# A decode layer on one core: the identity of the fold matmuls loaded once for eight, and w_down in blocks of 88, 96 and 128 partitions

## The chip, the core and the metric

The kernel runs on one core of a Trainium2 chip. The core has a matrix engine (TensorE, PE; its weight loads are shown on a row of their own, PEld), a vector engine (DVE), a scalar engine (ACT), GpSimd (POOL) and SyncE (SP), which here only issues DMAs. Sixteen DMA engines move data from the chip's memory (HBM) into the on-chip memory of 128 partitions. The engines run side by side and wait for each other by semaphores. The metric is the device time of one execution in microseconds (us), taken as the median of several runs.

## What is computed

One decode step (one token, width 640) of an attention block with cached keys and values, and a gated MLP behind it. Cut to what matters:

```python
def _A_ref(x, k_cache, v_cache, wq, wo):           # 32 heads of 128, 4096 cached positions
    q = (x @ wq).reshape(B, Sq, Hq, Dh).transpose(0, 2, 1, 3)
    scores = jnp.einsum("bhqd,bhkd->bhqk", q, k) * (Dh ** -0.5)
    p = _softmax(scores, axis=-1)
    o = jnp.einsum("bhqk,bhkd->bhqd", p, v)
    return o.transpose(0, 2, 1, 3).reshape(B, Sq, Hq * Dh) @ wo

def _B_ref(x, w_gate, w_up, w_down):               # 640 -> 1728 -> 640
    g = jnp.einsum("bsd,df->bsf", x, w_gate)
    u = jnp.einsum("bsd,df->bsf", x, w_up)
    h = _gelu(g) * u
    return jnp.einsum("bsf,fd->bsd", h, w_down)

h = x + _A_ref(_layernorm(x), A_k_cache, A_v_cache, A_wq, A_wo)
h2 = h + _B_ref(_layernorm(h), B_w_gate, B_w_up, B_w_down)
```

All inputs are bf16. Keys and values are 33.6 MB each, wq and wo 5.2 MB each, w_gate, w_up and w_down 2.2 MB each: 84.2 MB, each byte used once.

## The kernel before

The program is written out instruction by instruction: a small class (`Sched`) collects the operations of each engine in the order in which they are to run, with the semaphore values that each waits for, and emits them at the end. Nothing reorders them afterwards.

**Loads.** All large loads are issued from SP, in one order: wq; K of groups 0 and 1; V of group 0; then V and K of the further groups in turn; wo in two parts with the last V between them; w_gate, w_up; w_down; at the end the result. The 32 heads are worked in eight groups of four. A group's K (4 MB, two buffers `kbuf`) has 128 partitions, 32 for each head, with 128 positions in each; V likewise (`vbuf`). A load waits for its buffer: K's for the last product of the group two before, V's for the last value matmul of the group two before. The MLP's weights lie in the buffers that the caches leave: w_gate and w_up in `kbuf`, w_down (`wd_sb`) in `vbuf`.

**Scores.** For each group there are four pieces of 32 positions. `mult` (L339) multiplies K by the query on DVE, 128 x 4096 elements into `prod` (three buffers). `fold` (L348) sums over the head's 128 elements, 16 at a time: eight matmuls with the identity `Ibf` as the stationary operand add eight slices of `prod` into one PSUM bank `pf`. Each of the eight is a weight load of the same identity and a matmul. `red` (L355) sums the remaining 16 on DVE. `top`, `turn`, `head` and `soft` make the softmax's maximum and the exponentials (ACT, L384). `values` (L395) multiplies by V, `extract` (L410, L413) and `column` (L418) bring the result into columns, `project` (L601) multiplies by wo. The last group takes its values in `values_last` (L403).

**MLP.** `up` (L648) makes one column of 128 hidden units per matmul group: for each of the five slices of the input (`NC_D`) and each of the `NF` = 14 columns one matmul with 128 x 128 weights, first for w_gate (`pg`), then for w_up (`pu`). The columns follow the layout of w_down: `WD_PARTS` = (5, 4, 3, 1) are blocks of 128 partitions in which each partition holds 5, 4, 3 or 1 consecutive rows of w_down, 13 columns (`NFT`) in all, 1664 rows. The 14th column is the last 128 hidden units, of which 64 (`FREM`) are not in the others. Their 64 rows of w_down come in eight small loads (L581), each of four partitions with two rows (`NRR`) of 640 elements, to partitions of `wd_sb` that POOL has set to zero (L577). Since these rows lie otherwise than the column of hidden units, the column is brought to their places by L666 on DVE, a small matmul L670 (`rest`) and a copy L672, with the help of `hsum`, `hrow` and `hcol`, made in the prologue (L225 to L232).

The hidden units go through the GELU on DVE and ACT (L655 to L664) into `hm`. `down` (L686) then multiplies: for each of 15 columns of `wd_sb` four matmuls of 160 output elements each, into four partition quarters of `pd`, in the order: blocks of 5 and 4, the two of the small loads, blocks of 3 and 1. The small matmul L670 comes after the first five columns. L690 copies the result, L692 stores it.

Of the kernel before, what the change touches and what calls it, by code (L numbers as in the profile page):

```python
# [5 lines left out]
FP32 = mybir.dt.float32  # L6
BF16 = mybir.dt.bfloat16
ALU = mybir.AluOpType
ACTF = mybir.ActivationFunctionType
AX = mybir.AxisListType  # L10

D = 640
H = 32
DH = 128
SK = 4096
DF = 1728
# [7 lines left out]
NG = H // HG  # L24
# [6 lines left out]
NW = 4  # L31
HW = H // NW
DJ = 128 // HW
NFT = 13
NF = NFT + 1
WD_PARTS = (5, 4, 3, 1)

WD_COLS = []
for _n in WD_PARTS:
    _b = 128 * len(WD_COLS)  # L40
    WD_COLS += [(_b, _n, _i) for _i in range(_n)]
FREM = DF - NFT * 128
NRR = 2
NRP = FREM // NRR // 2
NRK = 32 + NRP
WIDE = 32


# [65 lines left out]
def bass_sequential_preLN__gqa_block_cached__glu_gated_geglu__decode_kernel(  # L114
# [12 lines left out]
    S = Sched(nc)  # L127

    def sb(name, shape, dt):
        return nc.alloc_sbuf_tensor(name, shape, dt)  # L130
# [5 lines left out]
    vbuf = [sb("vbuf%d" % i, [128, R, DH], BF16) for i in range(2)]  # L136

    def over(name, base, shape):
        return nc.alloc_sbuf_tensor_at(name, shape, BF16, offset=nc.lookup_mloc(base).addr)
# [2 lines left out]
    wo_sb = over("wo_sb", arena, [128, NW, HW, D])  # L142
    wg_sb = over("wg_sb", kbuf[NG % 2], [128, NC_D, DF])
    wu_sb = over("wu_sb", kbuf[(NG + 1) % 2], [128, NC_D, DF])
    wd_sb = over("wd_sb", vbuf[NG % 2], [128, NFT + NRR, D])

    NPR = 3
    prod = [sb("prod%d" % i, [128, RP, DH], BF16) for i in range(NPR)]
# [33 lines left out]
    r_t = sb("r_t", [128, NF], FP32)  # L182
    gu = sb("gu", [128, NF], FP32)
    hm = sb("hm", [128, NF], BF16)
    hq = sb("hq", [128, NRR], BF16)
    hr = sb("hr", [128, NRR], BF16)
    hcol = sb("hcol", [128, NRR], FP32)
    hrow = sb("hrow", [128, 128], BF16)
    o_sb = sb("o_sb", [128, D // 4], BF16)
    hx = sb("hx", [128, 32, NC_D], FP32)  # L190
    m32 = sb("m32", [128, 32], FP32)
# [2 lines left out]
    part = sb("part", [128, 128], FP32)  # L194
    eps = sb("eps", [128, 1], FP32)
    ones_bf = sb("ones_bf", [128, 128], BF16)
    I32 = sb("I32", [128, 128], FP32)
    Ibf = sb("Ibf", [128, 128], BF16)
    pf = [nc.alloc_psum_tensor("pf%d" % i, [128, 512], FP32) for i in range(2)]
# [3 lines left out]
    pz = nc.alloc_psum_tensor("pz", [128, 512], FP32)  # L203
# [17 lines left out]

    t_e4 = S.op("vector", lambda v: v.reduce_sum(
        e4[:, :], I32[:, :].rearrange("p (j i) -> p j i", j=4), axis=AX.X), [t_i32])
    hsum = hx[:, :, :].rearrange("p a b -> p (a b)")[:, 0:2 * NRP]
    t_hsum = S.op("vector", lambda v: v.reduce_sum(  # L225
        hsum, I32[:, 128 - FREM:128].rearrange("p (r i) -> p r i", i=NRR), axis=AX.X))
    t_hrow = S.op("vector", lambda v: v.memset(hrow[:, :], 0.0))
    t_hrow = S.op("vector", lambda v: v.tensor_copy(
        hrow[:, 0:64].rearrange("p (b r) -> p b r", b=2)[:, :, 0:NRP],
        hsum.rearrange("p (b r) -> p b r", b=2)), [t_hsum, t_hrow])  # L230
    t_hcol = S.op("vector", lambda v: v.reduce_sum(
        hcol[:, :], I32[:, 128 - FREM:128].rearrange("p (r i) -> p i r", i=NRR), axis=AX.X))  # L232
    t_m32 = S.op("vector", lambda v: v.reduce_sum(
        m32[:, :], I32[:, :].rearrange("p (j i) -> p i j", j=4), axis=AX.X))
    S.op("vector", lambda v: v.reduce_sum(
# [3 lines left out]
    a = S.op("vector", lambda v: v.reduce_sum(  # L239
        jred[:, :], I32[:, :].rearrange("p (j c) -> p j c", c=HW), axis=AX.X))  # L240
    b = S.op("vector", lambda v: v.reduce_sum(
        cred[:, :], I32[:, :].rearrange("p (j c) -> p c j", c=HW), axis=AX.X))
# [11 lines left out]
    kfree, vfree = [None] * NG, [None] * NG  # L254
# [45 lines left out]
    a = None  # L300
    for c in range(NC_D):
        a = S.op("tensor", lambda t, c=c: t.matmul(
            pm[:, c:c + 1], x_sb[0:1, c::NC_D], ones_bf[0:1, 0:1],
            start=(c == 0), stop=(c == NC_D - 1), skip_group_check=True),
            [d_x, t_onebf], token=(c == NC_D - 1))
# [23 lines left out]
    fold_done, red_done = {}, {}  # L329
# [7 lines left out]
    def mult(g, s):  # L337
# [3 lines left out]
            in1=qb[:, g, :].unsqueeze(1).to_broadcast([128, RP, DH]), op=ALU.mult),  # L341
            [d_k[g], t_qb[g], fold_done.get(n - NPR)])

    def fold(g, s, t_mult):
        n = g * NP + s
        W = 512 // RP
        for j in range(DH // W):
            fold_done[n] = S.op("tensor", lambda t, j=j: t.matmul(  # L348
                pf[n % 2][:, :], Ibf[:, :], prod[n % NPR][:, :, j * W:(j + 1) * W],
                start=(j == 0), stop=(j == DH // W - 1)),  # L350
                [t_mult, t_ibf, red_done.get(n - 2)], token=(j == DH // W - 1))

    def red(g, s):
# [99 lines left out]
    for n in range(NG - 1):  # L453
        w = (n - 3) // 2 if n >= 3 and n % 2 else None
        p, o = n - 1, n - 2
# [60 lines left out]
    g = NG - 1  # L516
    w = NW - 1
    p, o = g - 1, g - 2
# [45 lines left out]
    def load_wo(lo, hi):  # L564
# [9 lines left out]
                  [0, 5], [kfree[NG - 2]])  # L574
    d_wu = pieces("wu", wu_sb, B_w_up[:, :].rearrange("(p c) n -> p c n", c=NC_D),
                  [0, 5], [kfree[NG - 1]])
    t_zr = S.op("gpsimd", lambda g: g.memset(wd_sb[0:64, NFT:NFT + NRR, :], 0.0), [vfree[NG - 2]])  # L577
    rows = B_w_down[NFT * 128:DF, :].rearrange("(b e j i) n -> b j e i n", b=2, j=4, i=NRR)
    for h in range(2):
        for j in range(4):  # L580
            d_wdr = S.dma("sync", "wdr", lambda s, h=h, j=j: s.dma_start(  # L581
                wd_sb[32 * h + j:32 * h + NRP:4, NFT:NFT + NRR, :], rows[h, j]), [t_zr])
    d_wd = []
    for i, n in enumerate(WD_PARTS):
        s0 = len(d_wd)
        tok = S.dma("sync", "wd%d" % i, lambda s, s0=s0, n=n: s.dma_start(
            wd_sb[:, s0:s0 + n, :],
            B_w_down[128 * s0:128 * (s0 + n), :].rearrange("(p i) n -> p i n", i=n)), [vfree[NG - 2]])
        d_wd += [tok] * n
    d_wd += [d_wdr] * NRR  # L590


    pp = pf[0]
# [14 lines left out]
    for i in range(w - 1):  # L608
# [8 lines left out]
    b = project(w)  # L617
    t_h = S.op("vector", lambda v: v.scalar_tensor_tensor(
        out=h32[:, :], in0=x32[:, :], scalar=1.0, in1=pp[:, 0:NC_D * WIDE:WIDE], op0=ALU.mult, op1=ALU.add,
# [3 lines left out]
    pd = pf[1]  # L623
    NQ = D // 4
# [13 lines left out]
    def up(ps, w, d_w):  # L638
        b = None
        for c in range(NC_D):  # L640
            for s in range(NF):
                first = c == 0 and s == 0
                last = c == NC_D - 1 and s == NF - 1
                part = w[:, c, DF - 128:DF]
                if s < NFT:
                    b0, n, k = WD_COLS[s]
                    part = w[:, c, b0 + k:b0 + 128 * n:n]
                b = S.op("tensor", lambda t, s=s, c=c, part=part, first=first, last=last: t.matmul(  # L648
                    ps[:, s * WIDE:(s + 1) * WIDE], part, hln[:, c:c + 1].to_broadcast([128, WIDE]),
                    start=first, stop=last, skip_group_check=True), [t_hln, d_w[c]], token=last)  # L650
        return b
# [3 lines left out]
    a = S.op("vector", lambda v: v.tensor_copy(g_t[:, :], pg[:, 0:NF * WIDE:WIDE]), [t_g])  # L655
    a = S.op("vector", lambda v: v.tensor_mul(t1[:, :], g_t[:, :], g_t[:, :]), [a])
    a = S.op("vector", lambda v: v.tensor_mul(t2[:, :], t1[:, :], g_t[:, :]), [a])
    a = S.op("vector", lambda v: v.scalar_tensor_tensor(
        out=t3[:, :], in0=t2[:, :], scalar=GELU_C1, in1=g_t[:, :], op0=ALU.mult, op1=ALU.add), [a])
    a = S.op("scalar", lambda a: a.activation(e_t[:, :], t3[:, :], ACTF.Exp, scale=-2.0 * GELU_C0), [a])  # L660
    a = S.op("vector", lambda v: v.tensor_scalar(d_t[:, :], e_t[:, :], 1.0, 0.0, ALU.add, ALU.add), [a])
    a = S.op("vector", lambda v: v.reciprocal(r_t[:, :], d_t[:, :]), [a])
    a = S.op("vector", lambda v: v.tensor_mul(gu[:, :], g_t[:, :], r_t[:, :]), [a])
    t_hm = S.op("vector", lambda v: v.tensor_mul(hm[:, :], gu[:, :], pu[:, 0:NF * WIDE:WIDE]), [a, t_u])  # L664

    a = S.op("vector", lambda v: v.tensor_tensor(  # L666
        out=hq[:, :], in0=hcol[:, :], in1=hm[:, NFT:NF].to_broadcast([128, NRR]), op=ALU.mult), [t_hm, t_hcol])

    def rest():
        b = S.op("tensor", lambda t: t.matmul(  # L670
            pz[:, 32:32 + NRR], hrow[:, :], hq[:, :], start=True, stop=True), [a, t_hrow])
        return S.op("vector", lambda v: v.tensor_copy(hr[:, :], pz[:, 32:32 + NRR]), [b])  # L672

    def down(s, j):
        if s >= NFT:
            return hr[0:NRK, s - NFT:s - NFT + 1], wd_sb[0:NRK, s, j * NQ:(j + 1) * NQ]
        return hm[:, s:s + 1], wd_sb[:, s, j * NQ:(j + 1) * NQ]

    n = sum(WD_PARTS[0:2])
    order = list(range(n)) + list(range(NFT, NFT + NRR)) + list(range(n, NFT))  # L680
    for i, s in enumerate(order):
        if s == WD_PARTS[0]:
            t_hr = rest()
        for j in range(4):
            last = i == len(order) - 1
            b = S.op("tensor", lambda t, s=s, j=j, last=last: t.matmul(  # L686
                pd[32 * j:32 * j + 1, 0:NQ], *down(s, j),
                start=False, stop=last, skip_group_check=True),
                [t_hr if s >= NFT else t_hm, d_wd[s]], token=(last and j == 3))
    t_o = S.op("vector", lambda v: v.tensor_copy(o_sb[:, :], pd[:, 0:NQ]), [b])  # L690
    d_o = S.dma("sync", "out", lambda s: s.dma_start(
        out[0, 0, :].rearrange("(j i) -> j i", j=4), o_sb[0:128:32, :]), [t_o])  # L692
# [32 lines left out]
```

## Time and profile before

| what | value |
|---|---|
| median of 3 runs | 203.9 us (203.71 to 204.09) |
| span of the profiled execution | 202.3 us |
| TensorE busy | 155.4 us (77%), weight loads 71.0 us (35%) |
| DVE busy | 116.4 us (58%) |
| ACT, POOL busy | 30.7 us, 2.4 us |
| read from HBM | 84.23 MB, 416 GB/s over the span |
| mean granted TensorE clock | 0.930 |
| eight fold matmuls (L348) at the full clock | 1.85 us |
| issue of the eight small loads on SP | 5.10 us, from 175.80 |
| issue of the four large w_down loads | 1.86 us, from 180.94 |

The span runs from the first to the last instruction of one profiled execution; the runs' time has some 1.6 us more around it. Busy shares are means over very different stages: up to some 167 us the groups of K and V pass through, then wo and the MLP's weights come in while TensorE works in short stretches with waits between. The granted clock is 1.00 for most of the first part and 0.50 from 181 us to the end.

### The profile page before, as it was taken

The page shows a single profiled execution, that of the slowest core. Times are in us where ns is not written, and L with a number is a line of the kernel's source. Part 1 is how long each engine was busy: PE and PEld are TensorE (multiplying, and loading weights), DVE is VectorE, ACT ScalarE, POOL GpSimd, SP SyncE. Part 2 cuts the span into 40 slices and gives each one's busy share as a digit, 9 for nine tenths or more (in the row PEclk, how much of TensorE's full clock was granted, in tenths as well). Part 3 has the DMA queues.
Part 4 walks back from the last instruction along what each step waited for, and adds up shares of the span by engine and source line. Part 5 has one row for each costly group of instructions (what it writes and reads, how often), then busy time and mean ns, then how long its engine had stood idle before and what let it go on. Part 6 is the DMA issues. An engine that isn't in the chain of part 4 may idle for free.

```text
span 202.3 us, 2515 instructions
## 1 busy us (share of the span) xinstructions
PE 155.4 (77%) x1084; PEld 71.0 (35%) x1084; DVE 116.4 (58%) x153; ACT 30.7 (15%) x110; POOL 2.4 (1%) x8
## 2 busy tenths in 40 slices
PE   1005349689959997996899499979777999978675
PEld 1001013233323432432343134324323344667562
DVE  6200087998097919953993488569999513301121
ACT  2002200007000600420060004200604004000000
POOL 1000000000000000000000000000000000200000
PEclk9999999999979999999999979999999999985555
DMA  7999999999999999999999999999999899999993
GB/s 259 437 437 415 421 441 473 428 415 415 418 453 460 421 416 415 424 449 447 428 428 415 424 447 447 421 434 415 428 444 441 380 429 461 441 383 437 434 388 117
DMA packets 3940, 84.38 MB, mean 417 GB/s; under 512 B 441, under 2 KB 570, under 8 KB 986
## 3 DMA queue, kind: packets, MB, share of 16 engines
q1 hardware_dynamic: 3928, 84.23, 97.4%
q8 instruction: 8, 0.13, 0.3%
q14 instruction: 2, 0.02, 0.0%
q10 hardware_dynamic: 2, 0.00, 0.0%
HBM read 84.23 MB, written 0.00 MB: 416 GB/s over the span
## 4 chain that ended last, share of the span: by engine, by line
DMA 59%; DVE 24%; PE 15%; issue 1%; SPq 0%; DVEq 0%
DMA kbuf<-in_A_k_cache_dram 46%; DVE prod L339 16%; DMA wu_sb<-in_B_w_up_dram 13%; PE pf L348 8%; PE pu L395 4%; DVE sc L355 3%; DVE xz L413 2%; PE pu L648 1%; DVE xm L410 1%; PE pf L686 1%; PE pg L395 1%; DVE mx L363 0%; DVE mrow L372 0%; PE pm L367 0%; SPq L247 0%
## 5 line engine op out<-in xcount | busy, mean ns | idle before, releaser
L339 DVE TENSOR_TENSOR prod<-kbuf,qb 128x4096 bf16<-128x4096 bf16 x32 | 72.8, 2278 | 45.0 <-DMA kbuf<-in_A_k_cache_dram 45.0
L348 PE MATMUL pf<-prod,Ibf 128*128 128x512 bf16 x256 | 66.5, 408 | 23.0 <-DVE prod L339 22.9
L348 PEld LDWEIGHTS pf<-prod,Ibf 128*128 128x128 bf16 x256 | 24.4, 103 | 62.3 <-DVE prod L339 29.5
L395 PE MATMUL pg<-vbuf,P 128*16 128x512 bf16 x128 | 29.9, 379 | 0.0
L355 DVE TENSOR_REDUCE sc<-pf 128x32 f32<-128x512 f32 x32 | 21.6, 676 | 4.8 <-PE pf L348 4.7
L395 PE MATMUL pu<-vbuf,P 128*16 128x512 bf16 x96 | 22.2, 379 | 0.0
L318 PE MATMUL pq<-wq_sb,xb 128*128 128x512 bf16 x40 | 12.1, 441 | 12.3 <-DMA wq_sb<-in_A_wq_dram 11.1
L380 ACT ACTIVATE nb<-pm 128x4 f32<-128x4 f32 x8 | 1.4, 175 | 118.5 <-PE pm L377 118.5
L384 ACT ACTIVATE P<-sc,nb 32x128 bf16<-32x128 f32 x32 | 18.6, 580 | 0.9
L395 PEld LDWEIGHTS pg<-vbuf,P 128*16 128x16 bf16 x128 | 10.6, 89 | 14.5 <-issue 1.3
L395 PEld LDWEIGHTS pu<-vbuf,P 128*16 128x16 bf16 x96 | 8.1, 90 | 11.7 <-issue 1.7
L324 ACT CAST qb<-pq 32x128 bf16<-32x128 f32 x32 | 8.2, 258 | 15.8 <-PE pq L318 15.0
L318 PEld LDWEIGHTS pq<-wq_sb,xb 128*128 128x128 bf16 x40 | 3.8, 110 | 17.1 <-issue 12.8
L384 ACT ACTIVATION_READ_ACCUMULATOR P<-sc,nb 32x1 f32 x32 | 8.0, 251 | 0.0
L601 PE MATMUL pf<-aP,wo_sb 128*128 128x32 bf16 x160 | 7.1, 194 | 0.8 <-issue 0.6
L413 DVE TENSOR_REDUCE xz<-xm 16x128 f32<-16x512 f32 x7 | 7.3, 1044 | 0.2
L601 PEld LDWEIGHTS pf<-aP,wo_sb 128*128 128x128 bf16 x160 | 6.8, 131 | 1.5 <-issue 1.1
L403 PE MATMUL pq<-P,vbuf 128*128 128x32 bf16 x128 | 3.6, 188 | 1.4 <-DMA vbuf<-in_A_v_cache_dram 1.4
L410 DVE TENSOR_TENSOR xm<-pg,rmask 16x512 f32<-16x512 f32 x4 | 2.7, 670 | 3.4 <-PE pg L395 3.4
L293 ACT ACTIVATE ln<-pz,ln 128x1 f32<-128x1 f32 x2 | 0.5, 263 | 23.9 <-DVE ln L290 23.9
L403 PEld LDWEIGHTS pq<-P,vbuf 128*128 128x128 bf16 x128 | 3.5, 104 | 1.5 <-DMA vbuf<-in_A_v_cache_dram 1.5
L410 DVE TENSOR_TENSOR xm<-pu,rmask 16x512 f32<-16x512 f32 x3 | 1.9, 643 | 3.2 <-PE pu L395 3.2
(84 smaller groups left out, 56.4 us busy)
## 6 DMA issues: line engine op xcount, KB each, us to landing
kbuf<-in_A_k_cache_dram SPq DMA_DIRECT2D x8, 4096.0 KB, 25.2
vbuf<-in_A_v_cache_dram SPq DMA_DIRECT2D x8, 4096.0 KB, 22.8
wq_sb<-in_A_wq_dram SPq DMA_DIRECT2D x1, 5120.0 KB, 15.1
wo_sb<-in_A_wo_dram SPq DMA_DIRECT2D x1, 3840.0 KB, 28.7
wg_sb<-in_B_w_gate_dram SPq DMA_DIRECT2D x1, 2160.0 KB, 22.5
wu_sb<-in_B_w_up_dram SPq DMA_DIRECT2D x1, 2160.0 KB, 27.1
wo_sb<-in_A_wo_dram SPq DMA_DIRECT2D x1, 1280.0 KB, 17.8
wd_sb<-in_B_w_down_dram SPq DMA_DIRECT2D x1, 800.0 KB, 15.8
```

Source lines behind the costliest of these rows:

```text
L318: tok = S.op("tensor", lambda t, c=c, n0=n0: t.matmul(pq[:, :], xb[:, c, :], wq_sb[:, c, n0:n0 + HG * DH], start=(c == 0), stop=(c == NC_D ...
L324: t_qb[g] = S.op("scalar", lambda a, lo=lo, hi=hi, hh=hh: a.copy(qb[lo:hi, g, :], pq[lo:hi, hh * DH:(hh + 1) * DH]), [tok])
L339: return S.op("vector", lambda v: v.tensor_tensor(out=prod[n % NPR][:, :, :], in0=kbuf[g % 2][:, s * RP:(s + 1) * RP, :], in1=qb[:, g, :]. ...
L348: fold_done[n] = S.op("tensor", lambda t, j=j: t.matmul(pf[n % 2][:, :], Ibf[:, :], prod[n % NPR][:, :, j * W:(j + 1) * W], start=(j == 0) ...
L355: red_done[n] = S.op("vector", lambda v: v.reduce_sum(sc[g % 2][:, s * RP:(s + 1) * RP], pf[n % 2][:, :].rearrange("p (r w) -> p r w", r=R ...
L384: t_exp[g] = S.op("scalar", lambda a, lo=lo, hi=hi, h=h, hh=hh: a.activation(P4[g % 2][lo:hi, :, hh], sc[g % 2][lo:hi, :], ACTF.Exp, bias= ...
L395: t_pv[g] = S.op("tensor", lambda t, i=i, r=r, last=last: t.matmul(pv[g % 2][0:VM, :], P4[g % 2][:, r:r + VR, :], vbuf[g % 2][:, r:r + VR, :],
L403: t_pv[g] = S.op("tensor", lambda t, r=r: t.matmul(pq[:, 0:WIDE], vbuf[g % 2][:, r, :], P4[g % 2][:, r, :].unsqueeze(1).to_broadcast([128, ...
L410: a = S.op("vector", lambda v: v.tensor_tensor(out=xm[:, :, :], in0=pv[g % 2][0:VM, :].rearrange("p (r d) -> p r d", r=VR), in1=rmask[:, : ...
L413: t_ext[g] = S.op("vector", lambda v: v.reduce_sum(xz[g % 2][:, :], xm[:, :, :].rearrange("p r d -> p d r"), axis=AX.X), [a, t_acc[g - 2] ...
L601: tok = S.op("tensor", lambda t, c=c, cc=cc, first=first, last=last: t.matmul(pp[:, cc * WIDE:(cc + 1) * WIDE], wo_sb[:, w, c, cc::NC_D], ...
L648: b = S.op("tensor", lambda t, s=s, c=c, part=part, first=first, last=last: t.matmul(ps[:, s * WIDE:(s + 1) * WIDE], part, hln[:, c:c + 1] ...
```

## The change

Two things are changed.

In `fold` only the first of the eight matmuls brings its weights. The seven others are made as instructions by hand, with the flag that no weights are loaded, and use those that are there.

w_down is cut otherwise: a block of 88 partitions with four consecutive rows in each, one of 96 with one row, and blocks of 128 with 4, 3, 2 and 1 rows: 15 columns, 1728 rows. The 64 rows in eight small loads, POOL's memset, the rearranging of their hidden units (L666, L670, L672) and what the prologue prepares for it are gone. `up` works 15 columns with 128 weights each as before; of a column with 88 or 96 rows the rest of the result isn't read. `down` takes the columns in the order in which they are loaded, with 88, 96 or 128 partitions.

```diff
-NFT = 13
-NF = NFT + 1
-WD_PARTS = (5, 4, 3, 1)
+WD_PARTS = ((88, 4), (96, 1), (128, 4), (128, 3), (128, 2), (128, 1))
 
 WD_COLS = []
-for _n in WD_PARTS:
-    _b = 128 * len(WD_COLS)
-    WD_COLS += [(_b, _n, _i) for _i in range(_n)]
-FREM = DF - NFT * 128
-NRR = 2
-NRP = FREM // NRR // 2
-NRK = 32 + NRP
+_b = 0
+for _p, _n in WD_PARTS:
+    WD_COLS += [(_b, _n, _i, _p) for _i in range(_n)]
+    _b += _p * _n
+assert _b == DF
+NF = len(WD_COLS)
...
+    def again(t, out, lhsT, rhs, stop):
+        m = mybir.InstMatmult(
+            name=nc.get_next_instruction_name(), engine=mybir.EngineType.PE,
+            ins=[t.lower_ap(rhs), t.lower_ap(lhsT, for_matmul_weights=True)], outs=[t.lower_ap(out)],
+            start_tensor_calc=False, stop_tensor_calc=stop,
+            tile_size=(128, 128), tile_position=(0, 0), ldweights=False)
+        return t.add_instruction(m)
+
     def fold(g, s, t_mult):
...
-            fold_done[n] = S.op("tensor", lambda t, j=j: t.matmul(
-                pf[n % 2][:, :], Ibf[:, :], prod[n % NPR][:, :, j * W:(j + 1) * W],
-                start=(j == 0), stop=(j == DH // W - 1)),
+            def mm(t, j=j):
+                dst, src = pf[n % 2][:, :], prod[n % NPR][:, :, j * W:(j + 1) * W]
+                if j == 0:
+                    return t.matmul(dst, Ibf[:, :], src, start=True, stop=False)
+                return again(t, dst, Ibf[:, :], src, j == DH // W - 1)
+            fold_done[n] = S.op("tensor", mm,
                 [t_mult, t_ibf, red_done.get(n - 2)], token=(j == DH // W - 1))
...
-    t_zr = S.op("gpsimd", lambda g: g.memset(wd_sb[0:64, NFT:NFT + NRR, :], 0.0), [vfree[NG - 2]])
-    rows = B_w_down[NFT * 128:DF, :].rearrange("(b e j i) n -> b j e i n", b=2, j=4, i=NRR)
-    for h in range(2):
-        for j in range(4):
-            d_wdr = S.dma("sync", "wdr", lambda s, h=h, j=j: s.dma_start(
-                wd_sb[32 * h + j:32 * h + NRP:4, NFT:NFT + NRR, :], rows[h, j]), [t_zr])
     d_wd = []
-    for i, n in enumerate(WD_PARTS):
+    for i, (p, n) in enumerate(WD_PARTS):
         s0 = len(d_wd)
-        tok = S.dma("sync", "wd%d" % i, lambda s, s0=s0, n=n: s.dma_start(
-            wd_sb[:, s0:s0 + n, :],
-            B_w_down[128 * s0:128 * (s0 + n), :].rearrange("(p i) n -> p i n", i=n)), [vfree[NG - 2]])
+        b0 = WD_COLS[s0][0]
+        tok = S.dma("sync", "wd%d" % i, lambda s, s0=s0, b0=b0, p=p, n=n: s.dma_start(
+            wd_sb[0:p, s0:s0 + n, :],
+            B_w_down[b0:b0 + p * n, :].rearrange("(p i) n -> p i n", i=n)), [vfree[NG - 2]])
         d_wd += [tok] * n
-    d_wd += [d_wdr] * NRR
...
-                part = w[:, c, DF - 128:DF]
-                if s < NFT:
-                    b0, n, k = WD_COLS[s]
-                    part = w[:, c, b0 + k:b0 + 128 * n:n]
+                b0, n, k, _ = WD_COLS[s]
+                part = w[:, c, b0 + k:b0 + 128 * n:n]
...
-    n = sum(WD_PARTS[0:2])
-    order = list(range(n)) + list(range(NFT, NFT + NRR)) + list(range(n, NFT))
-    for i, s in enumerate(order):
-        if s == WD_PARTS[0]:
-            t_hr = rest()
+    for s, (_, _, _, p) in enumerate(WD_COLS):
         for j in range(4):
-            last = i == len(order) - 1
-            b = S.op("tensor", lambda t, s=s, j=j, last=last: t.matmul(
-                pd[32 * j:32 * j + 1, 0:NQ], *down(s, j),
+            last = s == NF - 1
+            b = S.op("tensor", lambda t, s=s, j=j, p=p, last=last: t.matmul(
+                pd[32 * j:32 * j + 1, 0:NQ], hm[0:p, s:s + 1], wd_sb[0:p, s, j * NQ:(j + 1) * NQ],
                 start=False, stop=last, skip_group_check=True),
-                [t_hr if s >= NFT else t_hm, d_wd[s]], token=(last and j == 3))
+                [t_hm, d_wd[s]], token=(last and j == 3))
```

More of the change, by code (lines that the diff above doesn't have):

```diff
@@ L144, in bass_sequential_preLN__gqa_block_cached__glu_gated_geglu__decode_kernel @@
     wu_sb = over("wu_sb", kbuf[(NG + 1) % 2], [128, NC_D, DF])
-    wd_sb = over("wd_sb", vbuf[NG % 2], [128, NFT + NRR, D])
+    wd_sb = over("wd_sb", vbuf[NG % 2], [128, NF, D])
     NPR = 3
@@ L184, in bass_sequential_preLN__gqa_block_cached__glu_gated_geglu__decode_kernel @@
     hm = sb("hm", [128, NF], BF16)
[L185 to L188, printed above, removed]
     o_sb = sb("o_sb", [128, D // 4], BF16)
@@ L223, in bass_sequential_preLN__gqa_block_cached__glu_gated_geglu__decode_kernel @@
         e4[:, :], I32[:, :].rearrange("p (j i) -> p j i", j=4), axis=AX.X), [t_i32])
[L224 to L232, printed above, removed]
     t_m32 = S.op("vector", lambda v: v.reduce_sum(
@@ L664, in bass_sequential_preLN__gqa_block_cached__glu_gated_geglu__decode_kernel @@
     t_hm = S.op("vector", lambda v: v.tensor_mul(hm[:, :], gu[:, :], pu[:, 0:NF * WIDE:WIDE]), [a, t_u])
[L666 to L677, printed above, removed]
-    n = sum(WD_PARTS[0:2])
-    order = list(range(n)) + list(range(NFT, NFT + NRR)) + list(range(n, NFT))
-    for i, s in enumerate(order):
-        if s == WD_PARTS[0]:
-            t_hr = rest()
+    for s, (_, _, _, p) in enumerate(WD_COLS):
         for j in range(4):
-            last = i == len(order) - 1
-            b = S.op("tensor", lambda t, s=s, j=j, last=last: t.matmul(
-                pd[32 * j:32 * j + 1, 0:NQ], *down(s, j),
+            last = s == NF - 1
+            b = S.op("tensor", lambda t, s=s, j=j, p=p, last=last: t.matmul(
+                pd[32 * j:32 * j + 1, 0:NQ], hm[0:p, s:s + 1], wd_sb[0:p, s, j * NQ:(j + 1) * NQ],
                 start=False, stop=last, skip_group_check=True),
-                [t_hr if s >= NFT else t_hm, d_wd[s]], token=(last and j == 3))
+                [t_hm, d_wd[s]], token=(last and j == 3))
     t_o = S.op("vector", lambda v: v.tensor_copy(o_sb[:, :], pd[:, 0:NQ]), [b])
```

## The prediction

> **What bounds the kernel now.** I read the page first: share of span, DMA row, queues.
>
> ```profile
> span 202.3 us, 2515 instructions
> ...
> DMA  7999999999999999999999999999999899999993
> ...
> DMA packets 3940, 84.38 MB, mean 417 GB/s; under 512 B 441, under 2 KB 570, under 8 KB 986
> ...
> q1 hardware_dynamic: 3928, 84.23, 97.4%
> q8 instruction: 8, 0.13, 0.3%
> ```
>
> SP's queue keeps the sixteen DMA engines busy 97.4% of the span, and no slice between the first and the last is below 8 tenths. The weights and caches come in one queue, in order: what lands last is set by the bytes of the slowest engine, not by when a load is issued. The DMA issues show the same: w_down's loads land 15.8 to 17.6 us after issue, because they stand behind w_up.
>
> Next the timeline of the end, weight loads of TensorE (start, us, what, in brackets the idle time before and its releaser):
>
> ```profile
> 194.84 2.42 PEld L648 LDWEIGHTS pu<-hln,wu_sb 128*128 128x128 bf16 x70 [1.52 <-DMA wu_sb<-in_B_w_up_dram]
> 197.69 0.49 PEld L686 LDWEIGHTS pf<-wd_sb,hm 128*1 128x1 bf16 x20 [0.44 <-DVE hm L664]
> 198.46 0.10 PEld L670 LDWEIGHTS pz<-hq,hrow 128*128 128x128 bf16 x1 [0.27 <-issue]
> 198.57 0.36 PEld L686 LDWEIGHTS pf<-wd_sb,hm 128*1 128x1 bf16 x16
> 199.20 0.10 PEld L686 LDWEIGHTS pf<-wd_sb,hr 48*1 48x1 bf16 x8 [0.27 <-issue]
> 199.57 0.23 PEld L686 LDWEIGHTS pf<-wd_sb,hm 128*1 128x1 bf16 x12 [0.26 <-DMA wd_sb<-in_B_w_down_dram]
> 199.94 0.09 PEld L686 LDWEIGHTS pf<-wd_sb,hm 128*1 128x1 bf16 x4 [0.15 <-DMA wd_sb<-in_B_w_down_dram]
> ```
>
> w_up's landing at 194.84 starts `pu`, and the last four matmuls of the down product wait for the last block of w_down until 199.94. Then come 0.36 us to PE's end, the 0.32 us copy L690 and the result's DMA. So two paths end together: DMA (199.94) and TensorE (60 matmuls of L686 and one of L670 from 197.69).
>
> Third, windows of the end: us, busy time of PE, PEld, DVE, ACT, POOL, clock, DMA share, GB/s:
>
> ```profile
> 198.50:198.75 0.25, 0.25 (x13) 0.24 (x13) 0.07 (x1) 0.00 (x0) 0.00 (x0) 0.50 0.64 256
> 198.75:199.00 0.25, 0.25 (x16) 0.18 (x8) 0.09 (x1) 0.00 (x0) 0.00 (x0) 0.50 0.49 184
> 199.00:199.25 0.25, 0.25 (x16) 0.05 (x8) 0.00 (x0) 0.00 (x0) 0.00 (x0) 0.50 0.52 190
> 199.25:199.50 0.25, 0.25 (x12) 0.05 (x8) 0.00 (x0) 0.00 (x0) 0.00 (x0) 0.50 0.15 51
> ```
>
> The engines do not stop together: 0.52 of 16 is 8.3 engines at work after 199.00, none after 199.50. I strung the trace's packet records into engines (each starts a packet as the one before ends). w_up's last packet ends on six engines at 192.5 to 192.7, on three at 193.2 to 193.5, on seven at 194.05 to 194.37. The seven are those that served a 16 KB instruction fetch before: the eight fetches of the q8 row start at 52, 85, 114, 151, 178, 185, 192 and 198 us, each at the end of a weight packet, and each holds its engine about 1.55 us. The four engines with the eight small loads (0.83 us of packets each) are not among the seven, but among the early ones; they finish w_down at 198.5 to 199.50, the seven at 199.1 to 199.46.
>
> **The change part by part.** *Identity loaded once per fold.* 32 folds lose 7 of 8 weight loads each, 224 of 103 ns:
>
> ```profile
> L348 PE MATMUL pf<-prod,Ibf 128*128 128x512 bf16 x256 | 66.5, 408 | 23.0 <-DVE prod L339 22.9
> L348 PEld LDWEIGHTS pf<-prod,Ibf 128*128 128x128 bf16 x256 | 24.4, 103 | 62.3 <-DVE prod L339 29.5
> ```
>
> A fold of eight takes 1.85 us at the full clock; without loads between nothing and 0.7 us (7 x 103 ns) goes. I take nothing from the end, as in the whole stretch to 167 us transfers cover it: a K or V load issued earlier stands behind others. The last such wait, V's load at 166.34, finds the queue with some 5 us of work (14 MB remain at 420 GB/s to 199.9, and 12.1 MB are issued from there on). Were that cover gone, four folds of the last group would give 0 to 2.8 us. Four DVE operations of the prologue go too, under the wait for the first K (25.6 us).
>
> It also shortens the instruction stream: 1084 matmuls with loads are 2168 records, and the changed kernel has 224 less, 20 more for ten matmuls in `up`, 2 less for L670. Eight fetches on about 2180 instructions are one for 256 to 270; some 1970 leave seven. Placed by the same counts, three or four come in the K stage, and the rest near 177, 183, 188 and 196 us. So again about seven engines are held before w_down is in.
>
> [...]
>
> *`up`, 15 columns for 14.* Five matmuls more in `pg` and `pu`, 36 ns each (70 in 2.52 us): `pg` is covered by the wait for w_up (1.4 us idle), `pu` adds 0.18 us. *Down.* 60 matmuls as before; L666, L670, L672 go, one matmul of 0.12 us on PE. First matmul at 197.87; at the pitch of 31 (12 in 0.37) to 39 ns (16 in 0.62) the last starts at 199.70 to 200.17, and with 0.3 us for its own run PE's path ends at 200.0 to 200.5, where it now ends at 200.30.
>
> *Issue.* Eight issues (5.1 us of SP) and the memset (1.16 us, POOL) go, and w_down is issued at 174.6 instead of 180.9. That moves nothing: w_up, ahead of it, lands at 194.8. Nothing new waits on SP; the result's DMA is still behind everything.
>
> *w_down over the engines.* This decides. The bytes are the same 2.21 MB; the shares are not. Start to start, packets cost 241 ns (6400 B), 194 (5120), 146 (3840), 99 (2560), 52 (1280). Before, a plain engine moves eight of each size but 2560: 8 x (241+194+146+52) = 5.06 us. After, blocks of 128 partitions give each engine 8 x (194+146+99+52) = 3.93 us, and the 96 rows 6 x 52 = 0.31. For the 88 partitions of 5120 B no row exists. Nearest rows: 128 partitions run as 8 on each of 16 engines, 4 as one on each of four (441 packets under 512 B are 16 completions for each of 25 loads, 4 for each of eight, and 9 for x and the result). Equal whole shares, then: 88 is 8 on 11 engines, which the 128-partition rows are nearest to; the bounds are 6 or 5 on all 16, and 11 on eight.
>
> [...] No run here shows the 11 yet.
>
> With 11: eleven engines carry 3.93 + 0.31 + 1.55 = 5.79 us, **0.73 us more** than a plain engine now, and the other five 4.24, 0.82 less. The engines of the small loads stay where they are (5.06 + 0.83 now). At most five of the seven held engines can be among the lighter five; the small loads' four are none of the seven, so at least two held engines are heavy. They end between 194.10 + 5.82 = 199.92 and 194.37 + 5.82 = 200.19 (0.03 us for completions); the middle, 200.07, is 0.57 us behind today's last packet (199.50). The last landing goes from 199.94 to 200.51, the last four matmuls follow as now, PE ends at 200.87.
>
> **Sum.** 0.00 (folds) + 0.57 (DMA path), PE's +0.18 hidden under it: profiled span 202.3 + 0.57 = 202.9. The runs' median is 203.9, 1.6 us above the span, for work around it that doesn't change: **204.5 us**. Its own range is 204.2 to 204.9.
>
> **Rivals.**
> *A. The late engines are the lighter five.* Should the fetches of the shorter stream fall on those five alone (or the sixth and seventh come after their engines are done), the shape pays back what a fetch costs: 1.55 us less on just these. Last is then an early-to-middle heavy engine, 193.49 + 5.82 = 199.31, and PE's path (200.0 to 200.5) decides. For it: 4.24 against 5.79 is just a fetch's length, and a fetch goes. Against: seven held engines now, and six fetches due by 189. Time 203.6 to 204.1, not slower; it decides as soon as no heavy engine is held.
> *B. 88 partitions spread over all sixteen,* 6 or 5 each: 5.40 us at most, +0.34 on a held engine, so the end moves by 0.14 to 0.30: 204.1.
> *C. Worse hits.* Two fetches on one engine, or 88 on eight engines (11 x 194 instead of 8): +1.3 to +2.1, 205.2 to 206.
> *D. The clock.* With shorter folds PE idles more; the granted clock already falls to 0.78 and 0.66 where it waits for K (55 to 60 us, 115 to 120). At half clock folds and values of one group need some 30 us against 20 us of loads, and engines run dry: several us slower. Against: it comes back within 3.4 us each time.
> *E. The loads are not dropped.* Then the folds stay as they are, and the end as forecast, since they were worth nothing.
>
> **Chances.** Forecast (with E) 0.58, A 0.22, B 0.10, C 0.06, D 0.04. A measurement tells 0.2%, 0.4 us, from no change. Slower: most of the forecast (0.53), a fifth of B, C and D: 0.65. Within: 0.05 of the forecast, 0.13 of A, 0.08 of B: 0.26. Faster: the low end of A, 0.09. The range 203.6 to 204.9 holds the forecast, A and B.
>
> **What would show it.** Right: L348's weight loads in 32 pieces and the folds shorter, with the same times of K's landings; w_up landing near 194.8; the last matmuls of the down product waiting for w_down until about 200.5; seven instruction fetches; a DMA share after 199.5 of two to six engines. Wrong: no wait of L686 for DMA (A), w_down landed by 199.8 (A or B), the wait for w_up ending elsewhere than at 194.8, or a granted clock of 0.5 before 180 us.

## The result and the profile after

The changed kernel takes **207.3 us** (median of 4 runs, 207.12 to 208.01) against 204.0 us for the kernel before beside it: ratio 1.0167, 95% interval 1.0143 to 1.019. It is slower, as forecast, but by 3.3 us and not by 0.6, outside the stated range.

The page of the profiled execution after:

```profile
span 205.9 us, 2294 instructions
...
DMA packets 4086, 84.37 MB, mean 410 GB/s; under 512 B 436, under 2 KB 661, under 8 KB 1133
...
q8 instruction: 7, 0.11, 0.2%
```

The span is 3.6 us longer. Seven instruction fetches are left, as worked out. The packets under 512 B say how many engines the loads ran on: 26 loads with 16 completions are 416, the 9 of x and the result make 425, and 11 remain for the load of 88 partitions. So it ran on eleven engines, as forecast.

The end's timeline, weight loads of TensorE (start, us; in brackets the idle time before and what ended it):

```profile
196.90 2.38 PEld L635 LDWEIGHTS pu<-hln,wu_sb 128*128 128x128 bf16 x75 [2.92 <-DMA wu_sb<-in_B_w_up_dram]
199.72 0.49 PEld L656 LDWEIGHTS pf<-wd_sb,hm 88*1 88x1 bf16 x20 [0.44 <-DVE hm L651]
201.21 0.36 PEld L656 LDWEIGHTS pf<-wd_sb,hm 128*1 128x1 bf16 x16 [0.99 <-DMA wd_sb<-in_B_w_down_dram]
202.34 0.23 PEld L656 LDWEIGHTS pf<-wd_sb,hm 128*1 128x1 bf16 x12 [0.78 <-DMA wd_sb<-in_B_w_down_dram]
203.15 0.10 PEld L656 LDWEIGHTS pf<-wd_sb,hm 128*1 128x1 bf16 x8 [0.57 <-DMA wd_sb<-in_B_w_down_dram]
203.55 0.09 PEld L656 LDWEIGHTS pf<-wd_sb,hm 128*1 128x1 bf16 x4 [0.30 <-DMA wd_sb<-in_B_w_down_dram]
```

These starts account for the whole loss. w_up starts `pu` at 196.90 instead of 194.84: 2.06 us, though w_up itself wasn't changed. From there to the last wait for w_down it is 6.65 us, before 5.10: 1.55 us. From that wait to the end of the span it is 2.35 us, as before (2.36). TensorE now waits for w_down at each of the four blocks of 128 partitions.

The windows of the end (busy time of PE, PEld, DVE, ACT, POOL; clock, DMA share, GB/s) tell why. Before:

```profile
192.00:194.00 2.00, 1.42 (x43) 1.31 (x40) 0.47 (x3) 0.00 (x0) 0.00 (x0) 0.50 0.94 385
194.00:196.00 2.00, 1.16 (x33) 1.16 (x34) 0.81 (x5) 0.22 (x1) 0.00 (x0) 0.50 1.00 413
196.00:198.00 2.00, 1.67 (x54) 1.56 (x55) 0.33 (x2) 0.00 (x0) 0.00 (x0) 0.50 1.00 399
```

After (here and below every line is one stretch of 2 us):

```profile
192.00:194.00 2.00, 2.00 (x69) 1.98 (x66) 0.00 (x0) 0.00 (x0) 0.00 (x0) 0.50 1.03 329
194.00:196.00 2.00, 0.09 (x4) 0.00 (x0) 1.29 (x7) 0.21 (x1) 0.00 (x0) 0.50 1.02 195
196.00:198.00 2.00, 1.10 (x35) 1.10 (x36) 0.00 (x0) 0.00 (x0) 0.00 (x0) 0.50 0.98 240
198.00:200.00 2.00, 1.67 (x58) 1.56 (x58) 0.17 (x1) 0.00 (x0) 0.00 (x0) 0.50 0.98 301
```

Read the last two columns together. The DMA engines are as busy as before (share 0.98 to 1.03), but move 195 to 301 GB/s where they moved 385 to 413. They are not idle and not unevenly loaded: each packet takes longer. The packet records agree. Between 194 and 198 us a packet of 5120 bytes (the load of 88 and the first of 128 behind it) took 247 to 565 ns, 347 in the median (before 196 to 207 ns), and one of 1280 bytes 113 in the median (55). w_up's last fifteen packets of 17280 bytes took 673 to 1468 ns (644); the first of them starts at 192.69, just behind the first packet of the load of 88 (192.55).

Longer packets are not all of w_up's 2.06 us. Its last packet ends at 195.51, 1.15 us later than before (194.36). From there to TensorE's start it is 1.39 us, before 0.48. In the other runs this gap is 0.8 to 1.0 us where a load of 64, 88 or 96 partitions comes behind w_up ahead of those of 128 (0.67 for the smallest), and 0.5 to 0.6 where none does. What the completion waits for there isn't shown.

### The profile page after: what moved, and what is told of

It reads as the page before. It is cut to its first block, busy times and chain, and to the rows that moved or that the text cites. A ratio compares the mean times of both kernels' runs of the same rounds, so it can differ in the third digit from the quotient of the medians.

```text
span 205.9 us, 2294 instructions
## 1 busy us (share of the span) xinstructions
PE 156.1 (76%) x1093; PEld 50.1 (24%) x869; DVE 115.5 (56%) x147; ACT 30.6 (15%) x110; POOL 1.2 (1%) x7
## 4 chain that ended last, share of the span: by engine, by line
DMA 50%; PE 24%; DVE 23%; SPq 1%; issue 1%
DMA kbuf<-in_A_k_cache_dram 37%; DVE prod L323 17%; DMA wd_sb<-in_B_w_down_dram 13%; PE pf L334 8%; PE pg L390 7%; PE pu L390 5%; DVE sc L350 4%; PE pf L343 2%; DVE xz L408 1%; SPq L576 1%; DVE xm L405 1%; PE pq L302 1%; PE pm L362 1%; DVE mx L358 0%; PE pf L656 0%
## 5 line engine op out<-in xcount | busy, mean ns | idle before, releaser
L334 PE MATMUL pf<-prod,Ibf 128*128 128x512 bf16 x224 | 57.2, 398 | 0.0
L343 PE MATMUL pf<-prod,Ibf 128*128 128x512 bf16 x32 | 13.1, 409 | 22.3 <-DVE prod L323 22.3
L390 PE MATMUL pu<-vbuf,P 128*16 128x512 bf16 x96 | 24.2, 404 | 0.0
L343 PEld LDWEIGHTS pf<-prod,Ibf 128*128 128x128 bf16 x32 | 3.1, 98 | 42.6 <-DVE prod L323 37.1
L390 PEld LDWEIGHTS pu<-vbuf,P 128*16 128x16 bf16 x96 | 8.6, 95 | 18.8 <-issue 9.8
L372 PEld LDWEIGHTS pm<-mrow,ones 1*128 1x128 f32 x16 | 2.3, 182 | 12.6 <-issue 12.6
L635 PE MATMUL pu<-hln,wu_sb 128*128 128x32 bf16 x75 | 2.5, 191 | 2.8 <-DMA wu_sb<-in_B_w_up_dram 2.8
```

The source lines that it names most:

```text
L334: return t.add_instruction(m)
L343: return t.matmul(dst, Ibf[:, :], src, start=True, stop=False)
L390: t_pv[g] = S.op("tensor", lambda t, i=i, r=r, last=last: t.matmul(pv[g % 2][0:VM, :], P4[g % 2][:, r:r + VR, :], vbuf[g % 2][:, r:r + VR, :],
```

## The experiments

All times are medians, all ratios are taken to the kernel before (203.8 us beside these runs), with 95% intervals.

**The fold alone.** The kernel before with the new `fold`:

```diff
-            fold_done[n] = S.op("tensor", lambda t, j=j: t.matmul(
+            def mm(t, j=j):
...
+                return again(t, dst, Ibf[:, :], src, j == DH // W - 1)
+            fold_done[n] = S.op("tensor", mm,
```

> The kernel before with the fold's identity loaded once per eight matmuls, w_down as before. Three theories of the 3.3 us that the change cost. P: the loads of 88 and 96 partitions are handed to the DMA engines in shares that write into the same parts of the on-chip memory, so their packets and those of w_up beside them take about twice as long. K: the recorded step, eleven engines carry more, only dearer than I made it. F: the fold's part costs, by the clock or by another place of the instruction fetches. P and K: 203.9 us (203.5 to 204.3), w_up landing at 194.8 as before. F: over 205.

203.97 us, 1.0012 (0.9999 to 1.0025): nothing that the runs can tell from noise. In its profiled execution w_up starts `pu` at 195.25, 0.4 us behind the expected 194.8; it is 195.03 in another run below that has no short load, so some tenths of a microsecond there mean nothing. Nor is a fold itself shorter. One fold in the timeline of the changed kernel, then the same one before:

```profile
155.27 0.39 PE L343 MATMUL pf<-prod,Ibf 128*128 128x512 bf16 x1 [0.77 <-DVE prod L323]
155.50 1.67 PE L334 MATMUL pf<-prod,Ibf 128*128 128x512 bf16 x7
```

```profile
155.25 1.90 PE L348 MATMUL pf<-prod,Ibf 128*128 128x512 bf16 x8 [0.78 <-DVE prod L339]
```

155.27 to 157.17 is 1.90 us for both: the seven weight loads of 103 ns that are gone had run beside the matmuls. Theory F, that the fold's part costs, falls.

**The blocks alone.** The changed kernel with a weight load before each fold matmul again (the diff above, backwards).

> The changed kernel with a weight load before each of the eight fold matmuls again: w_down's blocks alone. P and K: 207.0 to 207.6 us, w_up landing near 196.9 and packets of 5120 bytes at 300 to 560 ns, as with the whole change. F: 204.5 or less.

207.31 us, 1.0169 (1.015 to 1.0187): the whole loss, with w_up starting `pu` at 196.72. Its windows show the same low rate at full share:

```profile
194.00:196.00 2.00, 0.00 (x0) 0.00 (x0) 0.95 (x5) 0.21 (x1) 0.00 (x0) 0.50 0.97 207
196.00:198.00 2.00, 1.28 (x41) 1.28 (x42) 0.00 (x0) 0.00 (x0) 0.00 (x0) 0.50 1.01 232
```

**No load of 88 partitions.**

```diff
-WD_PARTS = ((88, 4), (96, 1), (128, 4), (128, 3), (128, 2), (128, 1))
+WD_PARTS = ((96, 2), (128, 5), (128, 4), (128, 2), (128, 1))
```

> The changed kernel with w_down in blocks (96,2), (128,5), (128,4), (128,2), (128,1): no load of 88 partitions, so by the shares seen so far all 16 engines carry the same, but one load still has fewer than 128 partitions (246 KB, against 573 KB in both blocks of the change). P: slower than before, by about the ratio of the bytes, 246 / 573 of 3.3 us, so 205.3 us (204.8 to 206.2), with w_up later than 195.2. K: no engine is heavier, 203.9 to 204.3, w_up at 194.8.

205.35 us, 1.0076 (1.0059 to 1.0093); w_up starts `pu` at 196.24. All 16 engines have six partitions of the first load here, and still:

```profile
196.24 2.41 PEld L635 LDWEIGHTS pu<-hln,wu_sb 128*128 128x128 bf16 x70 [2.79 <-DMA wu_sb<-in_B_w_up_dram]
```

```profile
194.00:196.00 2.00, 0.00 (x0) 0.00 (x0) 0.94 (x5) 0.21 (x1) 0.00 (x0) 0.50 0.93 257
```

So unequal shares (K) are not what costs; P's 205.3 was met.

**The short loads last.** The two loads are issued behind the four of 128, and used last.

```diff
+    late = [2, 3, 4, 5, 1, 0]
-    for i, (p, n) in enumerate(WD_PARTS):
+    for i in late:
+        p, n = WD_PARTS[i]
...
-    for s, (_, _, _, p) in enumerate(WD_COLS):
+    for s in order:
```

> The changed kernel with the loads of 96 and 88 partitions issued last, behind the four of 128, and used last. P: w_up is out of their reach and lands at 194.8 again; the two loads are still slow by themselves (8 packets of 5120 bytes at some 350 ns instead of 195, 1.2 us more), and stand at the very end: 205.5 to 206.5 us. K: as I forecast for the change, 204.2 to 204.9. If the loss comes from their being early alone, under 204.2.

206.53 us, 1.0145 (1.011 to 1.018), just at the upper end of P's range. The profiled execution is the longest of the four, 207.92 us, so its trace stands for that one. The timeline has the waits:

```profile
195.96 2.39 PEld L640 LDWEIGHTS pu<-hln,wu_sb 128*128 128x128 bf16 x75 [1.93 <-DMA wu_sb<-in_B_w_up_dram]
...
203.85 0.36 PEld L662 LDWEIGHTS pf<-wd_sb,hm 88*1 88x1 bf16 x16 [1.45 <-DMA wd_sb<-in_B_w_down_dram]
```

In this execution w_up came at 195.96, not at 194.8 as P has it, but not for short loads in its way: its packets keep 644 to 653 ns here, but for two right behind instruction fetches, at 1125 and 1192 ns. The later of these fetches is of 16 KB at 191.9. Its engine ended w_up at 195.40, the next one at 194.5; why it was so late isn't shown. The loss has moved to the load of 88, the last to land: 203.85 less 195.96 is 7.89 us, longer than the 6.65 of the whole change.

**The same bytes and places, cut by partitions or by rows.** In the kernel before, the first load of w_down is issued as two loads of 64 partitions:

```diff
+        for lo in ((0, 64) if i == 0 else (0,)):
+            hi = lo + 64 if i == 0 else 128
...
-            wd_sb[:, s0:s0 + n, :],
+                wd_sb[lo:hi, s0:s0 + n, :],
```

> The kernel before, its first load of w_down (128 partitions of 5 rows) issued as two loads of 64 partitions each: the same bytes, the same places, 16 engines with equal shares in both. P (packets slow down when a load's shares fall on memory that another engine is writing to): packets of 6400 bytes at 350 ns and more instead of 244, 205.2 to 207 us. K (unequal shares): 203.6 to 204.2 us, packets at 244 ns. A third reading, S: it is the number of loads or of completions that costs; then as the control run with two loads of 128 partitions.

206.57 us, 1.0152 (1.0111 to 1.0192). The control has two loads of 128 partitions, three rows and two:

```diff
+        for lo, hi in (((0, 3), (3, 5)) if i == 0 else ((0, n),)):
...
+                wd_sb[:, s0 + lo:s0 + hi, :],
```

> Control for the partition halves: the kernel before, its first load of w_down issued as two loads of all 128 partitions, three rows and two rows. P and K: 203.6 to 204.2 us, packets at the usual rate of their size (3840 bytes 149 ns, 2560 bytes 102 ns). S: as the partition halves.

203.88 us, 1.0002 (0.9993 to 1.0012). The windows, partition halves first:

```profile
194.00:196.00 2.00, 0.00 (x0) 0.00 (x0) 0.86 (x5) 0.21 (x1) 0.00 (x0) 0.50 0.93 226
196.00:198.00 2.00, 1.51 (x44) 1.51 (x45) 0.00 (x0) 0.00 (x0) 0.00 (x0) 0.50 1.04 229
```

```profile
194.00:196.00 2.00, 0.96 (x28) 0.97 (x29) 0.59 (x3) 0.20 (x1) 0.00 (x0) 0.50 1.00 396
196.00:198.00 2.00, 1.67 (x55) 1.56 (x56) 0.29 (x2) 0.00 (x0) 0.00 (x0) 0.50 1.05 412
```

This is the clearest pair: one load more in both, the same rows to the same places, 16 engines with equal shares. What differs is which engine writes to which partition, and the rate falls to 0.56 to 0.57 of the control's. The size of the packets differs too (3840 and 2560 bytes in the control), but the kernel before has them at 6400 bytes, as the partition halves do, at 244 ns. In the partition halves they took 422 ns in the median, up to 729. K falls, and so does S, the number of loads, as far as one load more can tell.

**The same rows over 128 partitions.** The changed kernel, its first two loads with the same rows of w_down, cut into 128 equal pieces.

```diff
+        e = p * n * D // 128
...
-            wd_sb[0:p, s0:s0 + n, :],
-            B_w_down[b0:b0 + p * n, :].rearrange("(p i) n -> p i n", i=n)), [vfree[NG - 2]])
+            wd_sb[:, s0:s0 + n, :].rearrange("p i n -> p (i n)")[:, 0:e],
+            B_w_down[b0:b0 + p * n, :].rearrange("r n -> (r n)").rearrange("(p e) -> p e", e=e)), [vfree[NG - 2]])
...
-                pd[32 * j:32 * j + 1, 0:NQ], hm[0:p, s:s + 1], wd_sb[0:p, s, j * NQ:(j + 1) * NQ],
+                pd[32 * j:32 * j + 1, 0:NQ], hm[0:p, s:s + 1], wd_sb[0:p, s % 2 if s < 4 else s, (j % 3 if s == 4 else j) * NQ:(j % 3 if s == 4 else j) * NQ + NQ],
```

`down` reads only what these loads fill, so it leaves out the right pairing of rows and hidden units.

> The changed kernel, the same rows of w_down in each of its six loads, but the first two spread over 128 partitions (3520 and 960 bytes each) instead of 88 and 96. Left out: the down product multiplies the rows of these two loads in the wrong places, so the output is not the reference's; every matmul is still there. P and K: the loss goes, 203.6 to 204.3 us, w_up landing at 194.6 to 195.3. Theory H (the rows' place in HBM or the sizes of the pieces): 206 to 207.5.

204.37 us, 1.0023 (1.0013 to 1.0033), just above P's range and far from H's. The rate is back:

```profile
194.00:196.00 2.00, 0.97 (x32) 0.92 (x30) 1.30 (x7) 0.21 (x1) 0.00 (x0) 0.50 1.02 391
```

```profile
195.08 2.40 PEld L636 LDWEIGHTS pu<-hln,wu_sb 128*128 128x128 bf16 x75 [1.14 <-DMA wu_sb<-in_B_w_up_dram]
...
200.52 0.09 PEld L657 LDWEIGHTS pf<-wd_sb,hm 128*1 128x1 bf16 x4 [0.30 <-DMA wd_sb<-in_B_w_down_dram]
```

So 2.9 us of the loss (207.3 less 204.37) are the shape of the two loads. The rest fits that all engines, those held by fetches too, now carry the 64 rows: from w_up's landing (195.08) to the last wait for w_down (200.52) it is 5.44 us, 0.34 more than before. From the packets 0.27 is worked out: eight each of 3520 and 960 bytes at some 135 and 40 ns, and of 2560 at 99, in place of eight of 6400 at 241.

**The eight small loads, spaced or adjacent.** The kernel before has four partitions at a distance of four in each. Here they are adjacent; the rows go along, so each row still lands where it did.

```diff
-    rows = B_w_down[NFT * 128:DF, :].rearrange("(b e j i) n -> b j e i n", b=2, j=4, i=NRR)
+    rows = B_w_down[NFT * 128:DF, :].rearrange("(b j e i) n -> b j e i n", b=2, j=4, i=NRR)
...
-                wd_sb[32 * h + j:32 * h + NRP:4, NFT:NFT + NRR, :], rows[h, j]), [t_zr])
+                wd_sb[32 * h + 4 * j:32 * h + 4 * j + 4, NFT:NFT + NRR, :], rows[h, j]), [t_zr])
```

> The kernel before; its eight small loads still take four partitions each, on four engines, with the same rows going to the same places in sum, but each takes four adjacent partitions instead of four at a distance of four. P: the four packets of a load fall on one part of the memory, 2560 bytes take 200 to 400 ns instead of 102; eight such in a row cost four engines 0.8 to 2.4 us: 204.5 to 206.3 us. K and H: nothing differs, 203.6 to 204.1 us.

204.22 us, 1.0017 (1.0003 to 1.003). The direction is P's, the size is not (it expected 204.5 or more): packets of 2560 bytes took up to 191 ns, but 105 in the median. The four engines come to these loads up to a microsecond apart, so by P they would meet only in part. The load behind suffers as well: 51 of its 128 packets of 6400 bytes took over 260 ns, before 2.

Then the same with only the places of writing changed (the first changed line of the diff left as it was):

> As the run with small loads to adjacent partitions, but each small load reads just the rows that it reads in the kernel before; only where they are written differs. Left out: the right order of the 64 rows, so the output is not the reference's. If the place of writing decides (P): as that run, some packets of 2560 bytes at 130 to 190 ns, 203.9 to 204.5 us. If the place of reading decides: all packets at 102 to 107 ns and 203.6 to 203.9 us.

204.45 us, 1.0029 (1.0019 to 1.0039); packets of 2560 bytes at 102 to 245 ns, and again 51 of 6400 bytes over 260. So the place of writing decides here, not that of reading.

**Two simpler ways to load the 64 rows,** both with the new fold.

```diff
-WD_PARTS = ((88, 4), (96, 1), (128, 4), (128, 3), (128, 2), (128, 1))
+WD_PARTS = ((64, 1), (128, 5), (128, 4), (128, 3), (128, 1))
```

> The changed kernel with w_down in blocks (64,1), (128,5), (128,4), (128,3), (128,1): 14 columns, the 64 rows in one load of 64 partitions, 82 KB on all 16 engines. P: a seventh of the bytes of the change's two short loads (573 KB, 3.3 us), so about 0.5 us lost: 204.0 to 204.8 us, its packets of 1280 bytes at 80 to 150 ns instead of 55. K: equal shares, 203.6 to 203.9.

204.58 us, 1.003 (1.0015 to 1.0045), as P had it, though its 1280-byte packets were slowed less (55 to 93 ns), and the 6400-byte packets behind them more (299 in the median). The second way has these 64 rows in eight loads of eight spaced partitions:

```diff
+            for q in range(8):
+                lo = 32 * (q // 4) + q % 4
...
+                    wd_sb[lo:lo + 29:4, 0, :], B_w_down[lo:lo + 29:4, :]), [vfree[NG - 2]])
```

> The same blocks, but the 64 rows in eight loads of eight partitions at a distance of four, as the kernel before spaced its small loads: by the shares seen so far eight engines, each writing to its own part of the memory. The identity is loaded once per fold, and the memset and the rearranging of the last hidden units are gone. P: packets of 1280 bytes at 55 to 60 ns, 203.5 to 204.0 us, so faster than the single load of 64 by 0.2 us or more. S (the number of loads costs): slower than the single load.

204.52 us, 1.0033 (1.0021 to 1.0046): the packets ran at 55 to 59 ns as P says, yet nothing is gained over the single load, and P's range is missed. In the load behind, sixteen packets of 6400 bytes, in eight pairs one after the other, took 354 to 769 ns. Why is open, and whether eight loads cost more than one isn't separated.

Both times lie within noise of the run with the same rows over 128 partitions (204.37 us, 1.0013 to 1.0033), which also puts the 64 rows on all engines. So most of what these two lose to the kernel before may be that, and the single load's hit on P's range is in part luck. No version beat the kernel before.

## Why the prediction was wrong in size

*Identity: worth nothing.* Right: 1.0012 (0.9999 to 1.0025) by itself. The instruction stream got shorter by one fetch, as counted (8 to 7). The fold at 155.3 us took 1.90 us with eight weight loads and with one.

*Eleven engines of eight partitions.* Right as to the number: 11 completions.

*The price of their packets.* **This is the step that failed.** The prediction costed the 88 partitions at 194 ns for 5120 bytes, the pace of loads over all 128 partitions ("which the 128-partition rows are nearest to"), and took that to be a matter of size alone. In the changed kernel the median was 347 ns, so eight such packets are some 2.8 us of an engine (an estimate from the two numbers), not 1.55. The runs showed that the pace belongs to the assignment of engines to partitions: with 88 and 96 partitions, or 64 of the same 128, packets took 1.7 to 2.1 times as long in the median (5120 bytes 347 ns against 198, 1280 bytes 113 against 55, 6400 bytes 422 against 244) with every engine busy; with the same rows over 128 partitions the rate is back (391 GB/s from 194 to 196 us, in the changed kernel 195). That two engines write to the same part of the memory is inferred from where the slow packets come; the trace has no row for a part of the memory, and which partitions would make up such a part isn't shown. The clearest evidence is the partition halves, 226 to 229 GB/s against 396 to 412 for the same bytes cut by rows; for 88 and 96 partitions it is the slow packets above. The prediction asked how many engines a load gets, and not where they write.

*"That moves nothing: w_up, ahead of it, lands at 194.8."* Wrong, and the larger part of the loss: 196.90. Ahead in the queue is ahead on each engine only. Engines that were done with w_up wrote short-load packets from 192.55 on, while others still wrote w_up until 195.51, and w_up's packets got slower with them; with the short loads issued last they kept their 644 ns.

*The held engines set the end* (+0.57 us). Not shown on the changed kernel, where the slow packets cover it. It was the forecast's only reason for a slower kernel; that the kernel came out slower had another cause, so the direction was in part luck. The 0.34 us of the run with 128 partitions is the size of such a shift.

*TensorE's path hidden under DMA.* Right: the down product waits four times for w_down, the last time until 203.55.

*Instruction fetches and TensorE.* The forecast charged a fetch to a DMA engine alone (1.55 us). Most likely too little, though it cost nothing here: TensorE's idle time in the last `project` (1.29 us, in the kernel before 0.58) fits a fetch (see the end).

*Rivals.* C's 88 on eight engines is refuted by the 11 completions, and its 205.2 to 206 us is too little as well; two fetches on one engine were not shown. B falls by the 11 completions too. A could not show itself, as slow packets and not held engines decide the end. E falls: `again` drops its loads, 32 of 256 are left. D's sign, a granted clock of 0.5 before 180 us, did appear, at 77 to 83 and 118 to 120 us. But the kernel before has it too, at 58 to 61 and 116 to 119, the fold alone cost nothing, and the blocks alone the whole loss; so D is not the cause.

## What to carry to other kernels

When the DMA share stays at 1.0 and GB/s falls (here from 385 to 413 down to 195 to 301), look for packets that take longer, and for loads with fewer than 128 partitions: cut a tensor by rows within the partitions, or spread a remainder over all 128, before cutting it by partitions (here 396 GB/s by rows, 226 by partitions). Here loads with few partitions cost their neighbours too: what stood ahead of them in the queue was still being written by the slower engines (the last packets of w_up took 673 to 1468 ns instead of 644). Before pricing a new shape by a row of another, ask what besides the size the row's pace came from.

## What the runs showed of the hardware

- Two loads of 64 partitions, each on all 16 engines, lowered the rate of all that ran beside them to 0.57 (226 GB/s against 396 for the same bytes cut by rows).
- In eight small loads of four partitions, adjacent or four apart differed by 0.17% (0.03 to 0.30) of the kernel, or 0.29% (0.19 to 0.39) where each load reads the same rows; the packets took 102 to 191 and 102 to 245 ns against 102 to 107.
- An instruction fetch of 16 KB held one DMA engine for about 1.55 us: in the kernel before the fetch at 191.89 took 1.08 us, and the packet of 17280 bytes behind it 1138 ns instead of 644.
- TensorE may wait for a fetch too. In the last `project` it stands idle for no reason that the trace names, 1.29 us in the changed kernel and 0.58 in the one before:

```profile
187.96 1.42 PE L590 MATMUL pf<-aP,wo_sb 128*128 128x32 bf16 x31 [1.29 <-issue]
```

```profile
187.89 0.78 PE L601 MATMUL pf<-aP,wo_sb 128*128 128x32 bf16 x15 [0.58 <-issue]
```

  In the twelve of the thirteen traces that show an idle time of 0.3 us or more there, it ends 2.3 to 2.7 us after the start of a fetch near 185 us (185.43 and 185.42 in these two). That it is the fetch that ends it is inferred from this. In the changed kernel the wait for w_up covered it.
- Weight loads of 128 columns before matmuls of 512 cost nothing that these runs tell: with 224 of them (103 ns each) gone, the fold at 155.3 us still took 1.90 us, and the kernel with the new fold alone 1.0012 (0.9999 to 1.0025) of its time.
